# Side work placed by DMA time as well, weights and values loaded through GpSimd's queue, values' high parts made on GpSimd

## The chip, the cores and the metric

The kernel runs on one core of a Trainium2 chip. The metric is device time in microseconds of one execution; smaller is better. The kernel before took 2106.71 us (median of 3 runs, 2103.33 to 2109.67).

In the profile, PE is TensorE (matmuls), PEld its weight loads, DVE is VectorE, ACT is ScalarE, POOL is GpSimd and SP is SyncE, which issues nearly all DMAs here; SPq stands for its queue.

## The reference

A squared-ReLU attention without softmax, a product with `u`, and a gated feed-forward layer with RMS norm, all in f32:

```python
scores = (1.0 / S) * np.matmul(z, z.transpose(0, 2, 1))   # z: 4 x 3008 x 64
attn = np.maximum(scores, 0.0) ** 2
out = np.matmul(attn, v)                                  # v: 4 x 3008 x 256
x = (u * out).reshape(B * S, D)                           # 12032 x 256
rms = np.sqrt(np.mean(x * x, axis=-1, keepdims=True) + 1e-06)
xn = x / rms * rms_g
g = xn @ w_gate                                           # 256 x 1536
silu = g * (1.0 / (1.0 + np.exp(-g)))
val = xn @ w_val
return (silu * val) @ w_out                               # 1536 x 256
```

## The kernel before

**Precision.** f32 products are made of reduced-precision (fp32r) matmuls: each operand is split into a high part (a cast) and a low part (the difference), and a product takes three matmuls: high times high, low times high, high times low. So every tile that PE reads has a "cast" and a "subtract" on some engine ahead of it: `vh` and `vl` are the two parts of the values v, `zst` holds both parts of z, `H` and `L` those of the attention weights.

**Attention.** Each of the 4 batches has 3008 columns of queries, taken as three pairs of 512-column blocks; that makes 12 pairs, numbered p = 0 to 11 (batch p // 3). "Second pairs" are p = 1, 4, 7, 10 and "third pairs" p = 2, 5, 8, 11. A pair walks over the 24 key tiles of its batch, one a step (`phase_a`). A step makes, for both blocks, the scores of the step after next (`emit_s`), the high and low parts of the next one (`emit_l`, lines 502 to 558), and the product of the present weights with v (`emit_av`, 12 matmuls for both blocks). z times z transposed is symmetric, so a pair stores weights that a later pair of the batch needs transposed (`kept`, `diag`: `keep_tile` and `keep_half`), and the later pair fetches them by a transposing DMA into one of 6 buffers `T` (`load_turned`, line 440, `load_half`, line 450). The later the pair, the more it fetches and the fewer score matmuls it has: a third pair fetches most of its weights.

**Feed-forward.** 12 blocks of 1024 tokens, 12 units each (`Unit`), each a seven-product scheme of combined gate and value weights (`wcomb`, `wu` when loaded) with combinations of x, then the product with w_out (`woh`, `wol`). While a block runs, the next block's norm and splits (`norm_jobs`, `split_jobs`) are put into its slots by `Beside.put`; a block has 36 slots.

**Side work.** While the attention runs, the next batch's z and v are loaded and split (`prep_stat`, `prep_v`), the weights are decoded from 64-bit floats (`decode`: a load, then an ACT `magnitude`, DVE bit operations, a POOL sum or split), the gate and value weights are combined (`prep_proj`: POOL `combine`s, ACT casts and POOL subtracts of the `put`s, and the stores to `wcomb`), and w_out is split (`prep_wout`).

**What sets the order.** Everything is recorded in program order; each engine works its instructions off in that order and waits at the first one that isn't ready. Where a piece of side work stands is chosen beforehand: `plan_loads` adds up, per step, the cost of the main work on DVE (`d`), ACT (`a`) and POOL (`g`); `put` (lines 1056 to 1071) takes for each piece the first step at which its engine has room; `plan_batch` (lines 1097 to 1119) does it for a batch's z and v, with the step by which each is needed. DMA time has no account of its own, and every load and store of this side work is an issue of SP, among the transposing loads.

Of the kernel before, what the change touches and what calls it, by code (L numbers as in the profile page):

```python
# [19 lines left out]
P = 128  # L20
# [10 lines left out]
def kernel(  # L31
# [120 lines left out]
    def decode(src, a, square, into):  # L152
# [48 lines left out]
    def prep_wout(f):  # L201
# [7 lines left out]
        tiles, load, ops = decode(rows, 2, square, lambda: "woh2" if f in (0, 4) else "x6")  # L209
# [17 lines left out]
    def prep_proj(j, pool, tags):  # L227
# [16 lines left out]
        def put(o, value):  # L244
            def both():
# [121 lines left out]
    def prep_v(b, g, place="start"):  # L367
        k0 = 2 * g
        r0 = b * S + k0 * P
        tiles = {}  # L370

        def load():
            view = tiles["raw"] = new_raw(place).rearrange("p (a d) -> p a d", a=2)
            if k0 + 2 < NK:
                nc.sync.dma_start(out=view, in_=v[r0:r0 + 2 * P, :].rearrange("(a p) d -> p a d", p=P))
            else:
                nc.sync.dma_start(out=view[:, 0, :], in_=v[r0:r0 + P, :])
                for h in range(2):
                    nc.sync.dma_start(out=view[h * TAIL:(h + 1) * TAIL, 1, :], in_=v[r0 + P:r0 + P + TAIL, :])
# [628 lines left out]
    load_of = {e: [0.0] * STEPS for e in "dag"}  # L1008
    span_of = [0.0] * STEPS

    def plan_loads():
# [5 lines left out]
        for p in range(NPAIR):  # L1017
            b, c0 = where(p)[:2]
            d = a = 0.0
            for i in range(NK):  # L1020
                kt, g = order(p)[i], p * NK + i
                for k in range(2):
# [20 lines left out]
                    if kc > c and keeps(b, c, kc):  # L1043
                        add("d", g - 1, 0.69)
                        d += 0.69
                    if kc == c and c and p > 0 and kt % 4 < 2:
                        add("d", g, 0.4)
                        d += 0.4
                d, a = d + SIDE[p > 0][0], a + SIDE[p > 0][1]
            add("d", (p + 1) * NK - 1 if p < NPAIR - 1 else STEPS - 1, 2.8)  # L1050

    SIDE = (0.55, 0.45), (0.55, 0.1)
    FILL = 0.9
    plan_loads()

    def put(seq, start, last=None):

        g = start
        for e, cost, gap, fn in seq:
# [3 lines left out]
            near = lambda k: range(max(k - 1, 0), min(k + 2, STEPS))  # L1063
            room = lambda k: sum(FILL * span_of[x] - load_of[e][x] for x in near(k))
            fits = (k for k in range(g, end + 1) if (load_of[e][k] == 0 if e == "g" else room(k) >= cost))
            g = next(fits, None) if last is None else next(fits, max(range(g, end + 1), key=room))
            load_of[e][g] += cost
            if e == "g" and cost > 3:
# [28 lines left out]
    def plan_batch(b, places):  # L1097
# [3 lines left out]
        for c in range(NC):  # L1101
            used = [i - LA for i in range(NK) if order(prev)[i] // 4 == c and not all(is_turned(prev, i, k) for k in range(2))]
            free = (prev * NK + max(used) + 1) if used else prev * NK + 1
            need = min(i - LA for i in range(NK) if order(here)[i] // 4 == c) + here * NK - 1
            todo.append((min(need, here * NK + NK - 1), free, "d", prep_stat, c))
# [4 lines left out]
        todo.sort(key=lambda t: t[:2])  # L1110
# [21 lines left out]
    def plan_part(part, g, last=None):  # L1132
        load, ops = part
        at_step(g, load)
# [4 lines left out]
    for j in range(NF // 4):  # L1139
# [4 lines left out]
        g = put(ends, max(g, ended[-1])) + 1  # L1144
# [3 lines left out]
    places.update({f: ((batch - 1) * NP - 1) * NK + 1 for f in (4, 5)})  # L1148
    plan_batch(batch - 1, places)
    for f in range(0, NF, 2):  # L1150
        ended.append(plan_part(prep_wout(f), max(g, ended[-2 if f < 8 else -1] + 1, ended[-1] if f == 8 else 0)))
        g += 4
# [10 lines left out]

    for p in range(1, NM):
        m = Beside(p - 1)
# [95 lines left out]
```

## Time and profile before

| | us |
|---|---|
| median of 3 runs | 2106.71 |
| the profiled execution's own time | 2107.22 |
| span of its trace, first to last instruction | 2105.4 |
| attention, up to the last gate of pair 11 | 1039.2 |

The profile's page gives busy time by engine and 40 slices of the span. Stretches by pair are cut at the first product of a pair's result with `u` (line 631, DVE), so pair 2 is 176.3 to 265.3 us, pair 5 is 437.3 to 528.8, pair 8 is 698.2 to 790.4; pairs 3, 4 and 7 are 265.3 to 350.9, 350.9 to 437.3 and 613.8 to 698.2. What follows 1039.2 us is the feed-forward layer. An idle time of PE after which a matmul waits for ACT has to be followed to what ACT itself waited for, and that to the queue on which the late transfer stood.

### The profile page before, as it was taken

Reading aid. Unit: us, or ns where it says so; the run is one execution under the profiler, and the core shown is the slowest. Engines: PE = TensorE matmul, PEld = TensorE weight load, DVE = VectorE, ACT = ScalarE, POOL = GpSimd, SP = SyncE. Lnnn points to the kernel's source line nnn. Section 1 sums busy time; section 2 is a strip of 40 time slices with the busy share of each in tenths; the row PEclk is TensorE's granted clock in tenths of the full one; section 3 lists DMA queues with packets and bytes.
Section 4 is the critical chain, followed back from the end, with each engine's and each line's share of the span. In section 5 each row is a group of like instructions: output and inputs, shape, how many; then the busy total and the mean of one; then the engine's idle time right before and its main releaser. Section 6 shows DMA issues by size and latency. Waiting matters only on the chain.

```text
span 2105.4 us, 27047 instructions
## 1 busy us (share of the span) xinstructions
PE 2026.7 (96%) x8912; PEld 1673.2 (79%) x8912; DVE 1605.4 (76%) x2644; ACT 1370.5 (65%) x2588; POOL 253.8 (12%) x412
## 2 busy tenths in 40 slices
PE   9999799987999789998999999999999999999999
PEld 7888688776877668877888888888888888888889
DVE  7888578665787568876788878788787888878776
ACT  7776487644876548765567666676666667666665
POOL 1202621046103361111000000000000000000000
PEclk9999999998999899999999999999999999999999
DMA  2476857899568974597634344443434434344443
GB/s 77 134 194 148 208 178 204 208 209 233 179 174 202 245 192 163 171 215 180 191 131 163 123 163 148 136 163 123 159 126 160 161 124 161 123 160 143 137 154 121
DMA packets 391982, 346.47 MB, mean 165 GB/s; under 512 B 254944, under 2 KB 303968, under 8 KB 391840
## 3 DMA queue, kind: packets, MB, share of 16 engines
q1 hardware_dynamic: 391840, 344.73, 55.8%
q8 instruction: 70, 1.15, 0.2%
q14 instruction: 72, 0.59, 0.1%
HBM read 190.78 MB, written 94.77 MB: 136 GB/s over the span
## 4 chain that ended last, share of the span: by engine, by line
PE 49%; ACT 1%; DVE 1%; DMA 1%; issue 0%; ACTq 0%; SPq 0%; DVEq 0%
PE ps L808 10%; PE ps L809 10%; PE ps L810 10%; PE py L836 6%; PE py L840 6%; PE py L837 6%; ACT s L815 1%; PE po L595 0%; PE po L596 0%; PE po L600 0%; ACT hH L820 0%; DVE xl L774 0%; DVE s L905 0%; DVE x L774 0%; DMA wu<-wc 0%; ACT s L899 0%
## 5 line engine op out<-in xcount | busy, mean ns | idle before, releaser
L595 PE MATMUL po<-H,vh 128*128 128x512 f32 (+1 forms) x1152 | 461.4, 401 | 64.4 <-ACT H L514 42.0
L596 PE MATMUL po<-H,vl 128*128 128x512 f32 (+1 forms) x1152 | 454.7, 395 | 0.0
L815 ACT COPY s<-ps 128x512 f32<-128x512 f32 (+1 forms) x432 | 249.7, 578 | 194.6 <-PE ps L810 194.6
L600 PE MATMUL po<-L,vh 128*128 128x512 f32 (+1 forms) x1104 | 345.1, 394 | 4.5 <-DVE L L525 4.4
L595 PEld LDWEIGHTS po<-H,vh 128*128 128x128 f32 x1152 | 223.1, 194 | 124.9 <-ACT H L514 48.7
L525 DVE TENSOR_TENSOR L<-r,H 128x512 fp32r<-128x512 f32 (+1 forms) x302 | 202.7, 699 | 132.2 <-ACT r L519 111.6
L820 ACT CAST hH<-s 128x512 fp32r<-128x512 f32 (+1 forms) x288 | 176.7, 614 | 176.5 <-DVE s L905 174.8
L825 DVE TENSOR_TENSOR hL<-s,hH 128x512 fp32r<-128x512 f32 (+1 forms) x288 | 196.3, 682 | 121.2 <-ACT hH L820 109.2
L487 ACT ACTIVATE r<-ps 128x512 f32<-128x512 f32 x322 | 178.2, 594 | 164.9 <-PE ps L476 148.4
L596 PEld LDWEIGHTS po<-H,vl 128*128 128x128 f32 x1152 | 223.0, 194 | 41.0
L600 PEld LDWEIGHTS po<-L,vh 128*128 128x128 f32 x1104 | 210.4, 192 | 51.0 <-DVE L L525 11.1
L525 DVE TENSOR_TENSOR L<-T,H 128x512 fp32r<-128x512 f32 (+1 forms) x250 | 185.6, 777 | 55.8 <-ACT H L514 54.2
L836 PE MATMUL py<-hH,woh 128*128 128x512 f32 (+1 forms) x576 | 221.7, 385 | 0.3 <-ACT hH L820 0.3
L837 PE MATMUL py<-hH,wol 128*128 128x512 f32 (+1 forms) x576 | 221.6, 385 | 0.0
L808 PE MATMUL ps<-x,wu 128*128 128x512 f32 x504 | 197.4, 392 | 0.9 <-DMA wu<-wc 0.6
L809 PE MATMUL ps<-x,wu 128*128 128x512 f32 x504 | 196.3, 390 | 0.7 <-DMA wu<-wc 0.7
L810 PE MATMUL ps<-x,wu 128*128 128x512 f32 x504 | 196.3, 389 | 0.0
L808 PE MATMUL ps<-xh,wu 128*128 128x512 f32 (+1 forms) x504 | 192.8, 383 | 0.4
L810 PE MATMUL ps<-xl,wu 128*128 128x512 f32 (+1 forms) x504 | 191.6, 380 | 0.0
L809 PE MATMUL ps<-xh,wu 128*128 128x512 f32 (+1 forms) x504 | 191.6, 380 | 0.0
L840 PE MATMUL py<-hL,woh 128*128 128x512 f32 (+1 forms) x576 | 174.8, 385 | 0.0
L514 ACT CAST H<-T 128x512 fp32r<-128x512 f32 (+1 forms) x254 | 143.1, 600 | 26.8 <-PE po L596 21.1
(99 smaller groups left out, 3454.7 us busy)
## 6 DMA issues: line engine op xcount, KB each, us to landing
wu<-wc SPq DMA_DIRECT2D x288, 448.0 KB, 3.9
kept<-halves SPq DMA_DIRECT2D x197, 256.0 KB, 2.1
raw<-in_v SPq DMA_DIRECT2D x44, 256.0 KB, 4.0
ux<-xg SPq DMA_DIRECT2D x22, 512.0 KB, 5.4
out_T<-y SPq DMA_DIRECT2D x44, 256.0 KB, 2.2
raw<-in_zT SPq DMA_DIRECT2D x38, 256.0 KB, 3.6
ux<-in_uT SPq DMA_DIRECT2D x38, 256.0 KB, 3.4
xg<-ux SPq DMA_DIRECT2D x22, 256.0 KB, 2.1
```

What stands on the lines that cost most here:

```text
L525: nc.vector.tensor_tensor(lo[:, :n], a[:, :n], f32(hi[:, :n]), op=ALU.subtract)
L595: nc.tensor.matmul(po[d][:, :n], wh[:, j, ds], hi[:, :n], start=(i == 0), stop=False)
L596: nc.tensor.matmul(po[d][:, :n], wl[:, j, ds], hi[:, :n], start=False, stop=(ends and lo is None))
L600: nc.tensor.matmul(po[d][:, :n], wh[:, j, ds], lo[:, :n], start=False, stop=ends)
L808: nc.tensor.matmul(ps[:, :n], wh[:, o, :], xh[:, :n], start=start, stop=False, skip_group_check=True)
L809: nc.tensor.matmul(ps[:, :n], wl[:, o, :], xh[:, :n], start=False, stop=False, skip_group_check=True)
L810: nc.tensor.matmul(ps[:, :n], wh[:, o, :], xl[:, :n], start=False, stop=stop, skip_group_check=True)
L815: nc.scalar.copy(s, ps[:, :self.n])
L825: nc.vector.tensor_tensor(lo[:, :self.n], s, f32(self.h[h][0][:, :self.n]), op=ALU.subtract)
L836: nc.tensor.matmul(acc[h, d][:, :n], woh[f // 4][:, f % 4, ds], hi[:, :n], start=(f == 0), stop=False)
L837: nc.tensor.matmul(acc[h, d][:, :n], wol[f // 2][:, f % 2, ds], hi[:, :n], start=False, stop=False)
L840: nc.tensor.matmul(acc[h, d][:, :n], woh[f // 4][:, f % 4, ds], lo[:, :n], start=False, stop=(f == NF - 1))
```

## The change

Five things:

1. **Queues.** The weights' loads and the stores to `wcomb` are issued by GpSimd instead of SP, and so are v's loads from the second batch on.
2. **v's high part.** From the second batch on, `vh` is cast by GpSimd in four pieces of 128 columns instead of by ACT in one instruction.
3. **The planner** keeps a fourth account, `q`, for DMA time (the transposing loads, the stores of `kept` and `diag`, the loads of u and z), and a load or a weight's store looks for a step with room in it; the room that an engine may be filled to is set for each account.
4. **Places.** A batch's raw buffers may be used from the middle of the second pair on (before: from the start of the third), and the first two z blocks of batches 2 and 3 are made in the second pair. The last batch's v moves largely from pair 8 to pair 9.
5. **w_out.** Rows 8 to 11 of w_out's 12 (two decodes of six) move into the first block of the feed-forward layer, into `T` buffers.

```diff
@@ decode
-            raw = (keep if tag[0] == "w" else moving).tile([P, a, b, 2], U32, tag=tag, name="wraw")
-            nc.sync.dma_start(out=raw.rearrange("p a b c -> p a (b c)"), in_=src.bitcast(U32))
+            pool = work if tag == "T" else moving if tag[0] == "x" else keep
+            raw = pool.tile([P, a, b, 2], U32, tag=tag, name="wraw", bufs=6 if tag == "T" else 1)
+            nc.gpsimd.dma_start(out=raw.rearrange("p a b c -> p a (b c)"), in_=src.bitcast(U32))
@@ prep_proj, store
-                        nc.sync.dma_start(
+                        nc.gpsimd.dma_start(
@@ prep_v
+        queue = nc.gpsimd if b else nc.sync
...
-                nc.sync.dma_start(out=view, in_=v[r0:r0 + 2 * P, :].rearrange("(a p) d -> p a d", p=P))
+                queue.dma_start(out=view, in_=v[r0:r0 + 2 * P, :].rearrange("(a p) d -> p a d", p=P))
...
-            nc.scalar.copy(hi, tiles["raw"])
+            if b == 0:
+                nc.scalar.copy(hi, tiles["raw"])
+                return
+            for a in range(2):
+                for k in range(0, D, PIECE):
+                    nc.gpsimd.tensor_copy(hi[:, a, k:k + PIECE], tiles["raw"][:, a, k:k + PIECE])
@@ plan_loads
+                    if i % 2 == 0 and is_turned(p, i, k):
+                        add("q", g - 7, 2.2)
...
-    FILL = 0.9
+    FILL = dict(d=0.93, a=0.93, q=1.05, g=1.0)
@@ plan_batch
+            if c < 2 and b > 1:
+                free -= NK
...
+            s = put([("q", 0.8, 0, None)], s, max(need - 6, s))
             load, one, two = prep(b, n, place=place)
             at_step(s, load)
...
-            h = put([("a", 0.6, 0, one), (e, 0.7 if e == "d" else 2.4, 1, two)], max(s + 2, free), last)
+            if e == "d":
+                h = put([("a", 0.6, 0, one), ("d", 0.7, 1, two)], max(s + 2, free), last)
+            else:
+                h = put([("g", 2.4, 0, one), ("g", 2.4, 0, two)], max(s + 2, free), last)
...
-        plan_batch(b, {f: (b * NP - 1) * NK + 1 for f in range(NF // 2)})
+        plan_batch(b, {f: (b * NP - 2) * NK + 6 for f in range(NF // 2)})
@@ the first block of the feed-forward layer
+    beside = [Beside(p) for p in range(NM - 1)]
+    for f, h in zip(range(8, NF, 2), (5, 15)):
+        load, ops = prep_wout(f)
+        at(("M", 0), h, load)
+        for k, (e, cost, _, fn) in zip((3, 4, 5, 6, 7, 8), ops):
+            at(("M", 0), h + k, fn)
+            beside[0].room[e, h + k] = beside[0].room.get((e, h + k), 0.0) - cost
```

Three places show what this makes of the order. First ACT in pair 5; L383 is the cast of v's high part, L514 (L521 in the change, as lines have shifted) the cast of attention weights `H` from a fetched tile, L250 (L251) that of a combined weight, L359 that of z. Before:

```order
L514 CAST H<-T 128x448
L383 CAST vh_4973<-raw 128x512
L359 CAST zst_4975<-raw 128x512
L359 CAST zst_4977<-raw 128x512
L514 CAST H<-T 128x512
L514 CAST H<-T 128x448
L250 CAST wohi<-w_4215 128x512
```

In the change, about the same place:

```order
L251 CAST wohi<-ws 128x512
L521 CAST H<-T 128x512
L521 CAST H<-T 128x448
L521 CAST H<-T 128x512
L521 CAST H<-T 128x448
L521 CAST H<-T 128x512
L521 CAST H<-T 128x448
L494 ACTIVATE T<-ps 128x256
```

The casts of v are gone from ACT; two of z's have moved ahead.

Second POOL at the end of the gate and value weights (the third group of them, j = 2): `ws<-` and `w<-` of L144 are combinations, `wolo` the low parts, `wc` the stores. Before, in pairs 7 and 8:

```order
L144 TENSOR_TENSOR w_6312<-w_6312,w_6350 128x128 x4
L144 TENSOR_TENSOR wolo<-w_6310,wohi 128x128 x4
L144 TENSOR_TENSOR w_5303<-w_6312,w_5303 128x128 x4
L144 TENSOR_TENSOR wolo<-w_6312,wohi 128x128 x4
L144 TENSOR_TENSOR wolo<-w_5303,wohi 128x128 x4
L144 TENSOR_TENSOR ws<-w_6310,w_5303 128x128 x4
```

In the change, all in the second half of pair 8 (L390 is now the cast of v's high part, L401 its low part, L377 v's load):

```order
L144 TENSOR_TENSOR w_7210<-w_7210,w_7353 128x128 x4
L377 DMA raw<-in_v 128x2x256
L144 TENSOR_TENSOR wolo<-w_7085,wohi 128x128 x4
L390 CAST vh_7798<-raw 128x128 x4
L256 DMA wc_80<-wohi 128x4x128
L256 DMA wc_80<-wolo 128x4x128
L144 TENSOR_TENSOR w_7056<-w_7210,w_7056 128x128 x4
L144 TENSOR_TENSOR wolo<-w_7210,wohi 128x128 x4
L401 TENSOR_TENSOR vl_7864<-raw,vh_7798 128x128 x4
L256 DMA wc_80<-wohi 128x4x128
L256 DMA wc_80<-wolo 128x4x128
```

Between two combinations there now stand a load, a cast, a low part and the stores, all in one queue.

Third ACT at the end of the feed-forward layer's first block, where the next block's x is cast (L769, in the change L776; L820 and L827 cast `hH`, L815 and L822 copy scores). Before, in three places, the last of which reads:

```order
L815 COPY s<-ps 128x512
L899 ACTIVATE s<-s 128x512
L769 CAST xh<-ux_10571 128x512
L769 CAST xh<-xc 128x512
L820 CAST hH<-s 128x512
```

In the change, in one:

```order
L906 ACTIVATE s<-s 128x512
L776 CAST xh<-ux_10638 128x512
L776 CAST xh<-ux_10640 128x512
L776 CAST xh<-xc 128x512 x2
L776 CAST xh<-ux_10638 128x512
L776 CAST xh<-xc 128x512
L776 CAST xh<-ux_10640 128x512
L827 CAST hH<-s 128x512
```

All seven casts of the next block (and on DVE their seven subtracts) have come to stand in the block's last slot, ahead of the cast for the last unit's product.

## Rows read from the trace of the kernel before

**Rows 1.** The page: PE's busy time, its granted clock and DMA by slice.

```profile
PE 2026.7 (96%) x8912; PEld 1673.2 (79%) x8912; DVE 1605.4 (76%) x2644; ACT 1370.5 (65%) x2588; POOL 253.8 (12%) x412
...
PEclk9999999998999899999999999999999999999999
DMA  2476857899568974597634344443434434344443
```

**Rows 2.** Windows: pairs 2, 3, 4, 5, 7, 8, feed-forward (columns: PE, PEld, DVE, ACT, POOL).

```profile
176.30:265.30 89.00, 76.51 (x329) 63.75 (x328) 56.62 (x85) 50.13 (x99) 44.55 (x72) 0.94 0.79 194
265.30:350.90 85.60, 85.06 (x376) 69.81 (x375) 68.38 (x109) 67.33 (x128) 15.61 (x25) 1.00 0.57 179
350.90:437.30 86.40, 80.91 (x342) 64.91 (x341) 62.17 (x107) 52.92 (x102) 5.82 (x12) 0.96 0.85 206
437.30:528.80 91.50, 73.70 (x309) 60.11 (x308) 57.78 (x83) 46.89 (x91) 59.89 (x92) 0.91 0.91 226
...
613.80:698.20 84.40, 79.84 (x342) 64.64 (x341) 61.95 (x100) 52.70 (x102) 24.46 (x40) 0.96 0.78 197
698.20:790.40 92.20, 75.31 (x310) 59.98 (x309) 58.49 (x88) 47.06 (x92) 44.06 (x72) 0.93 0.89 219
...
1039.20:2105.40 1066.20, 1061.65 (x4768) 886.48 (x4767) 845.13 (x1431) 693.05 (x1293) 0.00 (x0) 1.00 0.42 145
```

**Rows 3.** Timeline of PE in pair 5 (start, length, idle time before and releaser).

```profile
479.26 0.80 PE L595 MATMUL po<-H,vh 128*128 128x512 f32 x1 [7.67 <-ACT H L514]
```

**Rows 4.** Timeline of ACT just before.

```profile
477.03 0.62 ACT L383 CAST vh<-raw 128x512 fp32r<-128x512 f32 x1 [10.39 <-DMA raw<-in_v]
```

**Rows 5.** Timeline of SP's queue just before.

```profile
468.15 5.05 SPq L440 DMA_TRANSPOSE T<-kept  x2
473.25 0.57 SPq L375 DMA_DIRECT2D raw<-in_v  x1
```

**Rows 6.** Waits of ACT over the whole span (total, times, longest).

```profile
ACT vh L383 <- DMA raw<-in_v: 71.6, 18, 10.4
...
ACT T L487 <- DMA T<-diag: 40.0, 8, 8.1
...
ACT w L168 <- DMA wraw<-in_w_val: 6.0, 1, 6.0
```

**Rows 7.** Waits of PE in pair 8.

```profile
PE po L595 <- ACT H L514: 6.5, 6, 2.1
PE po L595 <- ACT H L512: 5.4, 2, 4.9
PE po L595 <- DVE H L529: 2.7, 1, 2.7
```

**Rows 8.** Timeline of ACT in pair 7.

```profile
677.61 0.62 ACT L250 CAST wohi<-ws 128x512 fp32r<-128x512 f32 x1 [4.19 <-POOL ws L144]
```

**Rows 9.** Groups by line: POOL's side work, and the feed-forward splits (busy, mean ns).

```profile
L394 POOL TENSOR_TENSOR vl<-raw,vh 128x128 fp32r<-128x128 f32 x180 | 109.9, 641 | 242.6 <-ACT vh L383 119.7 <-PE po L600 59.4 <-DMA kept<-halves 31.9
...
L144 POOL TENSOR_TENSOR wolo<-w,wohi 128x128 fp32r<-128x128 f32 x60 | 38.6, 673 | 72.2 <-ACT wohi L250 72.2
...
L144 POOL TENSOR_TENSOR ws<-w,w 128x128 f32<-128x128 f32 x24 | 16.8, 728 | 0.0
...
L774 DVE TENSOR_TENSOR xl<-ux,xh 128x512 fp32r<-128x512 f32 (+1 forms) x24 | 15.9, 664 | 2.0 <-ACT xh L769 2.0
...
L221 POOL TENSOR_TENSOR wol<-wraw 128x128 fp32r<-128x128 f32 x24 | 13.7, 569 | 1.9
```

**Rows 10.** Groups of DVE by form, 575 to 615 us (no POOL at work).

```profile
L525 DVE TENSOR_TENSOR L<-T,H 128x512 fp32r<-128x512 f32 x4 | 2.7, 684 | 0.0
```

**Rows 11.** The same, 500 to 525 us, with POOL at work.

```profile
L525 DVE TENSOR_TENSOR L<-T,H 128x512 fp32r<-128x512 f32 x6 | 5.2, 868 | 0.1
```

**Rows 12.** DMA issues over the span (KB each, median us from issue to landing).

```profile
raw<-in_v SPq DMA_DIRECT2D x44, 256.0 KB, 4.0
...
wc<-wohi SPq DMA_DIRECT2D x21, 256.0 KB, 3.4
```

More of the change, by code (lines that the diff above doesn't have):

```diff
@@ L207, in square @@
             return woh[f // 4][:, f % 4:f % 4 + 2, :]
-        tiles, load, ops = decode(rows, 2, square, lambda: "woh2" if f in (0, 4) else "x6")
+        tiles, load, ops = decode(rows, 2, square, lambda: "woh2" if f in (0, 4) else "x6" if f < 8 else "T")
         def high():
@@ L1007 @@
     STEPS = NPAIR * NK
-    load_of = {e: [0.0] * STEPS for e in "dag"}
+    load_of = {e: [0.0] * STEPS for e in "dagq"}
     span_of = [0.0] * STEPS
@@ L1044, in plan_loads @@
                         add("d", g - 1, 0.69)
+                        add("q", g, 0.8)
                         d += 0.69
@@ L1047, in plan_loads @@
                         add("d", g, 0.4)
+                        add("q", g, 0.5)
                         d += 0.4
+                    if i % 2 == 0 and is_turned(p, i, k):
+                        add("q", g - 7, 2.2)
+                    elif i % 2 == 0 and is_half(p, i, k):
+                        add("q", g - 4, 1.5)
                 d, a = d + SIDE[p > 0][0], a + SIDE[p > 0][1]
             add("d", (p + 1) * NK - 1 if p < NPAIR - 1 else STEPS - 1, 2.8)
+            for n in range(4):
+                add("q", p * NK + 8 + 2 * n, 0.9)
+                add("q", min(p * NK + NK + n % 2, STEPS - 1), 0.9)
+            for n in range(2):
+                add("q", p * NK + 8 + 2 * n, 0.9)
     SIDE = (0.55, 0.45), (0.55, 0.1)
-    FILL = 0.9
+    FILL = dict(d=0.93, a=0.93, q=1.05, g=1.0)
     plan_loads()
@@ L1062, in put @@
             g = min(g, end)
-            near = lambda k: range(max(k - 1, 0), min(k + 2, STEPS))
-            room = lambda k: sum(FILL * span_of[x] - load_of[e][x] for x in near(k))
+            wide = 3 if e == "q" else 1
+            near = lambda k: range(max(k - wide, 0), min(k + wide + 1, STEPS))
+            room = lambda k: sum(FILL[e] * span_of[x] - load_of[e][x] for x in near(k))
             fits = (k for k in range(g, end + 1) if (load_of[e][k] == 0 if e == "g" else room(k) >= cost))
@@ L1067, in put @@
             load_of[e][g] += cost
+            if fn is None:
+                continue
             if e == "g" and cost > 3:
@@ L1103, in plan_batch @@
             free = (prev * NK + max(used) + 1) if used else prev * NK + 1
+            if c < 2 and b > 1:
+                free -= NK
             need = min(i - LA for i in range(NK) if order(here)[i] // 4 == c) + here * NK - 1
-            todo.append((min(need, here * NK + NK - 1), free, "d", prep_stat, c))
+            todo.append((need if free >= prev * NK else prev * NK + 1, free, "d", prep_stat, c))
         for g in range(NK // 2):
@@ L1109, in plan_batch @@
             todo.append((need, free, "g", prep_v, g))
-        todo.sort(key=lambda t: t[:2])
+        todo.sort(key=lambda t: (t[0] - 12, t[1]))
         for need, free, e, prep, n in todo:
@@ L1133, in plan_part @@
         load, ops = part
+        g = put([("q", 1.5, 0, None)], g)
         at_step(g, load)
@@ L1143 @@
             g += 4
-        g = put(ends, max(g, ended[-1])) + 1
+        g = max(g, ended[-1])
+        for end in ends:
+            if end[0] == "a":
+                g = put([("q", 1.6, 0, None)], g)
+            g = put([end], g)
+        g += 1
     assert g < STEPS - 2 * NK, g
@@ L1147 @@
     places = {f"x{h}{k}": here for k in range(4) for h in "hl"}
-    places.update({f: ((batch - 1) * NP - 1) * NK + 1 for f in (4, 5)})
+    places.update({f: ((batch - 1) * NP - 2) * NK + 6 for f in (4, 5)})
     plan_batch(batch - 1, places)
-    for f in range(0, NF, 2):
-        ended.append(plan_part(prep_wout(f), max(g, ended[-2 if f < 8 else -1] + 1, ended[-1] if f == 8 else 0)))
+    for f in range(0, 8, 2):
+        ended.append(plan_part(prep_wout(f), max(g, ended[-2] + 1)))
         g += 4
@@ L1162 @@
         put([("a", 0.6, 0, one), ("d", 0.7, 0, two)], last + 17, STEPS - 1)
+    beside = [Beside(p) for p in range(NM - 1)]
[5 more added lines that the diff above has]
+            beside[0].room[e, h + k] = beside[0].room.get((e, h + k), 0.0) - cost
     for p in range(1, NM):
-        m = Beside(p - 1)
+        m = beside[p - 1]
         at(("M", p - 1), 0, lambda p=p: load_x(p))
```

4 lines of the change are left out of this document (2 added, 2 removed).

## The prediction

> **What bounds the kernel now.** I read the page first, then windows by pair, then the timeline around PE's longest idle times, then the waits. PE is busy for 96% of the span, so the kernel is bound by PE, and what can be won is PE's idle time and the time in which its clock is low [rows 1]. The slices place both: the granted clock, a mean of its two levels of 1.2 and 2.4 GHz, dips in the 10th and 14th slice, where the DMA row stands at 9. The windows give this by pair [rows 2]. Pair 3 has 376 matmuls in 85.6 us at full clock, 0.2277 us each, with PE idle for half a microsecond; I take that as an undisturbed pair's rate. At it, the matmuls of pair 2 (329) would take 74.9 us, of pair 4 (342) 77.9, of pair 5 (309) 70.4, of pair 7 (342) 77.9, of pair 8 (310) 70.6. They take 89.0, 86.4, 91.5, 84.4 and 92.2: losses of 14.1, 8.5, 21.1, 6.5 and 21.6 us, 72 together. The feed-forward layer has 1061.65 us of PE in 1066.2 and gives nothing back.
>
> What lies behind a loss is seen in pair 5. PE stands for 7.67 us [rows 3]; ACT, which makes its `H`, had stood for 10.39 us on the cast of a v block for the next batch, which nobody needed yet [rows 4]; and this block's load had been issued only 3.8 us before it, behind two transposing loads that held SP's queue for 5.05 us [rows 5]. So a piece of side work that isn't urgent blocks ACT in its order, and the block comes from the place of its load in SP's queue. Over the span ACT loses 71.6 us in 18 such waits, 40.0 in 8 waits for the diagonal tile and 6.0 in one for `w_val` [rows 6]. PE feels such a wait less some 3 us: 10.39 became 7.67 [rows 3, 4]. The loss is then larger than PE's idle time, since the clock comes back late: in pair 8, 21.6 us of loss against 14.6 us of waits, a factor of 1.5 [rows 2, 7].
>
> **The change part by part.** *v's casts leave ACT, v's loads leave SP.* In pairs 2, 5 and 8 ACT no longer meets a load of v at all. What is late next there is the diagonal tile, which still comes by SP: 40.0 us in 8, 5.0 each, less 3, times 1.5, is 3 us in each of the three pairs. Pair 8 also loses the wait behind a w_out load (inside the 5.4 us) and that on z (2.7) [rows 7], as both move to other pairs. So 11 of 14.1, 18 of 21.1 and 18.6 of 21.6: 48 us. If the planner's spreading leaves one wait of 10 us standing, (10 - 3) x 1.5 = 10 come off.
>
> *The weights' loads.* Pair 4's wait on `w_val`, 6.0 us, is half of its loss: 4 us back. In pair 7 the `wcomb` stores no longer stand in SP's queue ahead of the diagonal load; of 6.5 us I take 3 (0 to 6.5). The new order puts a load behind a POOL sum of some 2.5 us (4 x 641 ns [rows 9]); ACT waits of up to 4 us are covered by what PE has in hand, as one of 4.19 us behind POOL in pair 7 shows: that pair's only long PE idle is elsewhere [rows 8]. So nothing; with the cover gone, three loads at (6 - 3) x 1.5 = 4.5 each, 13 us.
>
> That is 55 us. Now what the change adds.
>
> *POOL's queue in pair 8* is the largest item. From S3's low part to the combination S4, on which ACT's last weight cast waits, POOL has three more low parts (4 in all, 4 x 673 ns = 2.7 us each), three combinations (4 x 728 ns = 2.9), one low part of v (2.6) and two casts of v. Such a cast isn't in the trace: it reads one operand of 128 x 128 where the nearest rows read two, at 569 to 641 ns a piece [rows 9]; below I can't exclude anything down to nothing, and take 2.1 us for four. Sum 26 us. Nine DMA issues stand between them. What one holds POOL for isn't in the trace either: SP holds 0.57 us for a plain load [rows 5]; the far end is that POOL stands until the transfer lands, 3.4 to 4.0 us [rows 12]. I take 0.7, near SP's. The plan gives 8 steps of 12 matmuls, 8 x 2.73 = 21.9 us. So ACT waits 26 + 9 x 0.7 - 21.9 = 10.4 us in pair 8; less 3, times 1.5: 11 us. At 0 an issue with free casts it is nothing, at 3.4 it is 48. Behind ACT's cast stand all the casts of `H`, so PE feels it.
>
> *v in pair 9.* The plan now makes these blocks exactly two steps ahead of use. At the start POOL has 8 loads in a row, then a cast and a low part, 8 x 0.7 + 4.7 = 10.3 us, behind pair 8's last low part and its two stores (2.7 + 2 x 0.7 = 4.1 us), and PE needs the block after 4 steps of 16 matmuls, 14.6 us. It just fits; I put 2 us there (0 to 27 at 3.4 us an issue).
>
> *DVE beside POOL.* The same subtract takes 684 ns without POOL and 868 with it [rows 10, 11]. Pairs 3, 6 and 9 now have POOL at work for half their length, where DVE is busy 68.4 of 85.6 us [rows 2]. Half of 109 instructions at 0.18 us more is 10 us of DVE; 17 us of its idle time take it, but not evenly. I take 1 us a pair, 3 in all (0 to 9). The Trainium skill (SBUF — State Buffer, section "SBUF: two separate sides") says that GpSimd and a VectorE instruction with two SBUF inputs lock each other out for a whole instruction; the longer subtract agrees in kind, though its 184 ns are less than a whole POOL piece of 641, so the sum stays with the rows.
>
> *Feed-forward, first block.* Two w_out decodes add 10 DVE and 4 ACT instructions, which push the next block's seven subtracts into the last slot. There, five more than before, 5 x 0.66 = 3.3 us [rows 9], stand ahead of what the last unit's product needs. PE has no other work then: 4 us (0 to 9).
>
> *DMA.* Transposing loads stay in the third pairs and PE will use them faster; with v's loads spread and the last group's stores now in pair 8 I put 4 us (0 to 20, the second rival).
>
> Sum: 11 + 2 + 3 + 4 + 4 = 24 us against 55, so 31 us fewer. The profiled execution took 2107.22 us, 0.5 above the median; 2107.2 - 31 = 2076, and I say 2075.
>
> **The rivals.** *GpSimd's queue becomes the bound* (slower). Its mechanism is the one of pair 8: with d us an issue, pair 8 costs 1.5 x (1 + 9d), pair 9 max(0, 10d + 7.4 - 14.6) by the sums above, and 11 us are fixed. At d = 2.1 this eats the 55; at d = 2.5 it is 35 + 18 + 11 = 64, 2116 us; at 3.4 it is 85, 2137. Against it: SP's 0.57 us; for it: nothing bounds a GpSimd issue from above but the landing. The Trainium skill (the same page and section) warns that a DMA issued from GpSimd waits while VectorE copies in its faster modes, as GpSimd writes the descriptors; no run here shows a GpSimd issue, and by that rule d would be longer than SP's.
>
> *The transfers themselves are the bound.* DMA is busy 79 to 91% of the third pairs [rows 2], so a load issued earlier may only make another one late. In pair 8 the busy time is 0.89 x 92.2 = 82 us, in pair 5 83, in pair 2 70. If these pairs shrink only as transfers leave them (by the order some 11, 15 and 9 us' worth), 35 come back instead of 48, and the costs of 24 and the gains of 7 beside them leave 18: 2089 us. For it: slices at 9. Against it: ACT's waits name v's loads, and none names the transposing ones [rows 6]. The Trainium skill (DMA: Bandwidth & Descriptors, section "Issuing engines are not separate DMA queues") says that issuing from more engines saves only the sequencer's issue time; here that time is 5.05 us for two loads ahead of one that ACT waits for [rows 5], so even by that rule the wait goes.
>
> *The costs don't come.* POOL's lag stays under ACT's cover, and the full 55 and pair 7's rest come back: 2047 us.
>
> *The waits only change place.* ACT meets z and weights instead of v, and the planner's rooms don't hold at run time: 2100 to 2112, no change.
>
> **How the numbers follow.** The forecast has 0.56 (2058 to 2085 by its own terms), the transfers 0.16, no costs 0.10, changed place 0.08, GpSimd as the bound 0.10. A measurement tells 0.3%, 6.3 us, from no change. Faster: 0.56 + 0.16 + 0.10 less a little of the second for terms at their far ends, 0.81; same 0.08; slower 0.11. The range reaches from under the case without costs to the far side of changed places: 2040 to 2108.
>
> **What would show it.** Right: no wait of ACT for v after the first batch; pairs 2 and 5 near 75 us with the granted clock at 0.97 or more; waits of ACT for POOL's `ws` or `w` of about 10 us in pair 8; issues that hold POOL under 1 us; a PE gap of a few microseconds near the end of the first feed-forward block. Wrong: waits for T from `kept` where v's were (the transfers), or POOL idle on its own issues while PE waits for `vh` or `vl` in pair 9 (GpSimd's queue). If pairs 2 and 5 keep over 10 us of their losses, the account of rows 3 to 5 fails.

## The result and the profile after

The changed kernel takes 2116.86 us (median of 6 runs, 2108.57 to 2119.69) against 2104.92 for the kernel before (median of 6): a ratio of 1.0051, with a 95% interval of [1.0035, 1.0067]. It is slower by half a per cent, where 2075 had been forecast, and lies outside the range of 2040 to 2108. The page of its profiled execution (span 2115.0 us; the columns as in [rows 1]):

```profile
PE 2030.0 (96%) x8912; PEld 1675.3 (79%) x8912; DVE 1640.5 (78%) x2644; ACT 1354.9 (64%) x2552; POOL 361.8 (17%) x658
...
PEclk9999999999899999999999999999999999999999
DMA  2466856997369985588644344443434434344443
```

One dip of the clock is left of two, in the 11th slice, which is pair 6. DVE is busy 35 us longer than in [rows 1], with the same 2644 instructions. The windows by pair show what that costs. After, pairs 4 to 9 and the feed-forward layer (length; PE, PEld, DVE, ACT, POOL, each busy time with its instructions; then the granted clock, DMA share, GB/s):

```profile
348.10:439.80 91.70, 79.95 (x341) 64.00 (x341) 64.13 (x101) 55.36 (x105) 21.56 (x35) 0.94 0.88 215
439.80:516.50 76.70, 70.41 (x309) 59.11 (x308) 52.49 (x84) 38.05 (x74) 44.18 (x83) 0.96 0.86 205
516.50:616.20 99.70, 87.98 (x374) 71.17 (x374) 82.50 (x109) 66.50 (x127) 29.33 (x72) 0.93 0.51 160
616.20:702.20 86.00, 80.81 (x342) 65.13 (x341) 64.81 (x100) 55.33 (x106) 21.97 (x34) 0.96 0.85 229
702.20:779.30 77.10, 70.25 (x309) 59.45 (x308) 54.40 (x81) 40.33 (x78) 47.27 (x80) 0.96 0.86 195
779.30:875.70 96.40, 90.06 (x374) 69.40 (x373) 85.43 (x113) 67.62 (x129) 55.07 (x99) 0.98 0.64 201
...
1043.70:2115.00 1071.30, 1063.41 (x4768) 887.38 (x4766) 851.49 (x1441) 695.80 (x1297) 9.64 (x18) 1.00 0.42 145
```

Pairs 6 and 9 of before, which [rows 2] leave out:

```profile
528.80:613.80 85.00, 84.47 (x373) 69.30 (x373) 68.64 (x113) 67.98 (x129) 5.20 (x8) 1.00 0.59 182
790.40:875.40 85.00, 84.48 (x374) 69.33 (x373) 70.04 (x112) 67.50 (x129) 11.72 (x16) 1.00 0.55 170
```

The third pairs 5 and 8 gave back 14.8 and 15.1 us (91.5 and 92.2 in [rows 2]). The pairs behind them took as much: pair 6 is 14.7 us longer and pair 9 11.4, with as many instructions on DVE, give or take four, but 13.9 and 15.4 us more of its busy time. Pair 4 is 5.3 us longer instead of 4 shorter, and the feed-forward layer 5.1 longer. The cuts of [rows 2] don't all lie at the same point: 265.3 us is the start of pair 2's first product with `u`, most others are its end, some 0.6 us later, and 176.3 lies 0.9 us ahead of pair 1's. Cut at the start of the first product in both kernels, pair 2 goes from 88.1 to 83.0 us and pair 3 from 84.9 to 87.0; the other differences stay.

What happened in pair 6 stands in four engines' timelines (start, length, engine; idle time before and releaser in brackets):

```profile
538.07 1.29 DVE L532 TENSOR_TENSOR L<-r,H 128x512 fp32r<-128x512 f32 x2
539.28 13.31 DVE L581 COPY halves<-r 128x1024 uint16<-128x1024 uint16 x2
552.51 0.68 DVE L501 TENSOR_TENSOR r<-ps,r 128x512 f32<-128x512 f32 x1
...
538.60 0.73 POOL L377 DMA_DIRECT2D raw<-in_v  x1 [14.60 <-ACT r L526]
539.33 0.99 POOL L390 CAST vh<-raw 128x128 fp32r<-128x128 f32 x4
540.30 1.29 POOL L401 TENSOR_TENSOR vl<-raw,vh 128x128 fp32r<-128x128 f32 x3
...
552.08 0.60 ACT L494 ACTIVATE r<-ps 128x512 f32<-128x512 f32 x1 [10.18 <-DVE halves L581]
...
553.84 1.22 PE L607 MATMUL po<-L,vh 128*128 128x512 f32 x2 [10.35 <-DVE L L532]
```

One 16-bit copy of DVE, of 0.69 us elsewhere, took 12.7 us (13.31 with the next one). It began 0.05 us before the end of a DMA issue of POOL, and ended only when POOL's stretch of 36 further pieces without a pause was over (551.4). ACT waited for DVE, PE for both, and the granted clock of the pair is 0.93, where it was 1.00. In pair 9 the same comes in small, eight times, of 2.0 to 2.3 us each; once here:

```profile
816.12 0.68 DVE L532 TENSOR_TENSOR L<-r,H 128x512 fp32r<-128x512 f32 x1
816.72 2.04 DVE L532 TENSOR_TENSOR L<-T,H 128x512 fp32r<-128x512 f32 x1
...
814.50 2.44 POOL L390 CAST vh<-raw 128x128 fp32r<-128x128 f32 x4
816.92 2.15 POOL L401 TENSOR_TENSOR vl<-raw,vh 128x128 fp32r<-128x128 f32 x4
```

In the trace of before no DVE instruction takes over 1.2 us; after, 18 do, 54.6 us together. They are called long below. The one just shown ends at 818.76, ahead of GpSimd's last subtract (819.07): VectorE got its turn here without a pause of GpSimd, while in pair 6 it came only behind the pause.

Waits of ACT after, over the whole span (total, times, longest); of v's 71.6 us of [rows 6] only 2.6 are left, in the first batch, and the diagonal tile's have grown by 10:

```profile
ACT T L494 <- DMA T<-diag: 50.5, 7, 11.5
ACT H L521 <- PE po L603: 36.9, 51, 3.2
ACT r L494 <- DVE halves L581: 30.8, 14, 10.2
ACT H L521 <- DMA T<-kept: 17.2, 9, 3.6
```

### The profile page after: what moved, and what is told of

It is laid out like the page before. It is cut to its first block, busy times and chain, and to the rows that moved or that the text cites. A ratio compares the mean times of both kernels' runs of the same rounds, so it can differ in the third digit from the quotient of the medians.

```text
span 2115.0 us, 27190 instructions
## 1 busy us (share of the span) xinstructions
PE 2030.0 (96%) x8912; PEld 1675.3 (79%) x8912; DVE 1640.5 (78%) x2644; ACT 1354.9 (64%) x2552; POOL 361.8 (17%) x658
## 4 chain that ended last, share of the span: by engine, by line
PE 50%; ACT 1%; DVE 1%; DMA 0%; issue 0%; ACTq 0%; DVEq 0%
PE ps L815 10%; PE ps L816 10%; PE ps L817 10%; PE py L843 6%; PE py L844 6%; PE py L847 6%; PE po L607 1%; PE po L603 1%; ACT s L822 1%; PE po L602 1%; DVE xl L781 0%; DVE s L912 0%; ACT hH L827 0%; DMA wu<-wc 0%; DVE x L781 0%; ACT s L906 0%
## 5 line engine op out<-in xcount | busy, mean ns | idle before, releaser
L822 ACT COPY s<-ps 128x512 f32<-128x512 f32 (+1 forms) x432 | 249.8, 578 | 194.5 <-PE ps L817 194.4
L532 DVE TENSOR_TENSOR L<-r,H 128x512 fp32r<-128x512 f32 (+1 forms) x302 | 220.2, 757 | 92.9 <-ACT r L526 72.1
L827 ACT CAST hH<-s 128x512 fp32r<-128x512 f32 (+1 forms) x288 | 176.8, 614 | 179.4 <-DVE s L912 177.7
L815 PE MATMUL ps<-x,wu 128*128 128x512 f32 x504 | 197.5, 392 | 1.6 <-DMA wu<-wc 1.3
L815 PE MATMUL ps<-xh,wu 128*128 128x512 f32 (+1 forms) x504 | 193.2, 383 | 3.2 <-DVE s L912 2.9
L521 ACT CAST H<-T 128x512 fp32r<-128x512 f32 (+1 forms) x254 | 145.4, 601 | 62.2 <-PE po L603 36.9
```

The source lines that it names most:

```text
L532: nc.vector.tensor_tensor(lo[:, :n], a[:, :n], f32(hi[:, :n]), op=ALU.subtract)
L815: nc.tensor.matmul(ps[:, :n], wh[:, o, :], xh[:, :n], start=start, stop=False, skip_group_check=True)
L822: nc.scalar.copy(s, ps[:, :self.n])
```

## The experiments

Experiments 1, 11 and 12 are small kernels of their own; all others start from the changed kernel. GpSimd does two new things in it, issues and casts; the experiments take them apart. Ratios are to the kernel before, with 95% intervals.

**1. Two streams by themselves.** A kernel in which 30 subtracts on VectorE run beside different streams of GpSimd.

```python
def dve(n=30):
    for _ in range(n):
        nc.vector.tensor_tensor(lo, a, f32(h), op=ALU.subtract)          # 128x512
phase([]); phase([subs] * 8); phase([casts, subs] * 6); phase([twos, subs] * 5)
phase([issue, subs] * 6); phase([casts] * 12); phase([issue] + [subs] * 8); phase([casts] + [subs] * 8)
```

> Computes nothing of the reference: seven times, 30 subtracts of 128x512 back to back on VectorE (0.69 us each alone) stand beside a stream of GpSimd instructions of 128x128, with both engines meeting ahead of each. Theory A (VectorE is starved where GpSimd goes from a one-input cast or a DMA issue to a two-input subtract): beside 32 subtracts the two engines take turns, no VectorE instruction over 1.2 us; beside groups of 4 casts and 4 subtracts, and of a DMA issue and 4 subtracts, about one of 1.5 to 2.5 us in each of the 6 groups; beside 4 two-input copies (x - 0) and 4 subtracts, none; beside casts alone, none; behind one issue, or 4 casts, with 32 subtracts, one of up to 14 us. Rival B (any unbroken stretch of GpSimd work slows VectorE alike): the same mean in all stretches of two-input work, 0.9 to 1.1 us, and none over 1.5.

Measured: the windows of the first three and of the two with issues (DVE, ACT, POOL; the few extra instructions are the meetings):

```profile
1.30:25.80 24.50, 20.78 (x32) 1.93 (x3) 0.29 (x2) 1.00 0.06 21
25.80:53.10 27.30, 24.68 (x33) 0.00 (x0) 26.93 (x34) 1.00 0.00 0
53.10:83.20 30.10, 22.68 (x32) 0.00 (x0) 29.82 (x50) 1.00 0.00 0
...
113.50:142.80 29.30, 28.28 (x32) 0.00 (x0) 18.99 (x32) 1.00 0.18 54
...
169.20:204.00 34.80, 33.81 (x32) 0.00 (x0) 14.51 (x35) 1.00 0.03 8
```

Beside 32 subtracts the engines take turns: 0.83 us an instruction of DVE, 0.90 a piece of POOL. Behind one issue, POOL does the same 32 at 0.45 us each, and one DVE instruction takes 13.75 us. In the six groups with an issue three take 2.57, behind every second issue. Behind the others the engines take turns, though GpSimd made no pause; its four subtracts then take 3.05 us instead of 1.69:

```profile
114.28 0.85 POOL L67 DMA_DIRECT2D load<-in_v  x1
115.15 1.69 POOL L54 TENSOR_TENSOR vl<-raw,vh 128x128 fp32r<-128x128 f32 x4
116.79 0.72 POOL L67 DMA_DIRECT2D load<-in_v  x1
117.53 3.05 POOL L54 TENSOR_TENSOR vl<-raw,vh 128x128 fp32r<-128x128 f32 x4
```

The three long instructions began 0.08 to 0.09 us before the end of an issue, those that took turns 0.13 to 0.14 us after it. Casts made none: half of theory A falls here, and so does B.

**2. Two inputs instead of a cast** (index expressions shortened).

```diff
-                    nc.gpsimd.tensor_copy(hi[:, a, k:k + PIECE], tiles["raw"][:, a, k:k + PIECE])
+                    nc.gpsimd.tensor_tensor(hi[...], tiles["raw"][...], zeros.to_broadcast([P, PIECE]), op=ALU.subtract)
```

> The high part of v is made by GpSimd as raw - 0 (two inputs) instead of as a cast (one input), at the same places and from the same queue. Theory A (starvation where GpSimd goes from one input to two): the 8 long VectorE instructions of pair 9 that begin beside a cast (2.0 us each instead of 0.69) become turns of 0.95, 8 x 1.1 = 9 us off pair 9 (96.4 to about 88); that of 12.7 us in pair 6 begins beside a DMA issue and may stay; total about 2108 against 2116.9. Rival B (GpSimd's amount of work is what counts): a piece takes 0.45 instead of 0.28 us, so pairs 6 and 9 get longer by 0 to 3 us, 2117 to 2122. Rival C (v comes late by GpSimd's queue): no change, 2115 to 2119.

Measured: 2128.86 us, 1.0112 [1.0099, 1.0125]; 19 long instructions, 75.0 us. Theory A expected pair 9 to recover; it took 110.1 us, and this stood in it:

```profile
816.73 18.32 DVE L535 TENSOR_TENSOR L<-r,H 128x512 fp32r<-128x512 f32 x1
```

So the change from a cast to two inputs isn't the cause. The long copy of pair 6, over 36 pieces as before, takes 14.66 us instead of 12.71: longer pieces make a longer wait. The 18.32 us cover 46 pieces up to GpSimd's next pause, where with casts VectorE had come in after three.

**3. The cast by ACT again.**

```diff
-            if b == 0:
+            if True:
                 nc.scalar.copy(hi, tiles["raw"])
                 return
```

> The cast of v's high part goes back to ACT, at the places where GpSimd had it; loads stay on GpSimd's queue. Theory A: no change from one input to two is left except behind DMA issues, and each low part waits for ACT's cast, which breaks GpSimd's runs: pair 6 from 99.7 to about 87 and pair 9 from 96.4 to about 88, together 20 us, less up to 10 where ACT waits for v again in the third pairs: 2097 to 2107. Rival B: the work on GpSimd falls by the casts (about a third of v's), pairs 6 and 9 shorter by some 8 together: 2109. Rival C: the loads are as late as before, pairs 6 and 9 keep their length: 2115 or more.

Measured: 2092.09 us, 0.9934 [0.9913, 0.9956]: faster than before, and faster than any theory had it (A from 2097). Pairs 6 and 9:

```profile
515.50:601.00 85.50, 84.97 (x374) 69.39 (x373) 73.60 (x109) 69.44 (x133) 31.69 (x48) 1.00 0.59 187
764.80:852.70 87.90, 85.10 (x373) 69.18 (x373) 75.29 (x114) 72.50 (x139) 42.53 (x60) 1.00 0.71 223
```

Eight long instructions are left (30.1 us), all beside issues of weights' stores. Pair 8 stays at 75.7 us though ACT casts again: v's casts needn't have left ACT. C falls.

**4. v's loads by SP, the cast by GpSimd.**

```diff
-        queue = nc.gpsimd if b else nc.sync
+        queue = nc.sync
```

> v's loads go back to SP's queue, casts stay on GpSimd, places as in the change. Theory A: the 12.7 us in pair 6 (begins beside the issue of such a load) goes or falls to groups of 2 us, pair 9 keeps its 8 instructions of 2 us, as they begin beside casts: pair 6 about 88 to 92, pair 9 about 95, total 2105 to 2110, if SP's queue is not blocked by a load that waits for its buffer (14.6 us on GpSimd in pair 6; on SP that would hold up the transposing loads, and pairs 3 and 6 would get longer). Rival C: both pairs fall to about 87, total 2095. Rival B: both pairs stay, 2115.

Measured: 2111.06 us, 1.0027 [1.0015, 1.0039]; 22 long instructions (56.4 us); pair 6 at 92.9, pair 9 at 95.6, close to what A said. The weights are still issued by GpSimd, one of them 7.0 us before pair 9's first instruction of 2.0 us.

**5. The stores by SP**, cast by ACT: in the store of the combined weights `nc.gpsimd.dma_start` becomes `nc.sync.dma_start`.

> v's high part cast by ACT (as in the last-but-one experiment, 2092 us) and the stores of the combined weights issued by SP again; the loads of v and of the weights stay on GpSimd's queue. Theory A (a VectorE instruction that comes while GpSimd is in a DMA issue is passed over by all that GpSimd does next): all 8 VectorE instructions over 1.2 us begin beside such a store (30 us together), so none is left; PE feels only that of 6.2 us in pair 8 (4.2 us idle): total 2084 to 2090. Rival B (amount of work): no change in them, 2092. Rival D (SP's queue): 42 more issues of 0.6 us on SP stand ahead of the diagonal tile's load, pairs 4 and 7 get longer by 2 to 4 us each: 2094 to 2100.

Measured: 2090.85 us, 0.9935 [0.9914, 0.9956]. The eight long instructions are gone, three others (9.4 us) stand behind v's issues. The time is the same as in 3, so what the eight cost can't be told in it.

**6. The weights' loads by SP too**: the same edit in `decode`.

> As the one before, and the weights' loads are issued by SP too; only v's loads stay on GpSimd's queue. In pair 4 the wait for the diagonal tile is 12.7 us with the cast on ACT (7.3 before the change), behind transposing loads that held SP for 5.8 and 8.4 us beside a weight's load from GpSimd's queue. If a load from the other queue is what stretches them, pair 4 falls by 4 to 8 us: 2082 to 2088. If the place that the planner gives to the weights' loads does it (now 10 to 15 us nearer to the diagonal tile), pair 4 stays near 95 and the total at 2086 to 2094.

Measured: 2085.31 us, 0.9903 [0.9883, 0.9923]. Pair 4 falls from 98.6 us in the kernel of 5 to 87.3:

```profile
344.50:431.80 87.30, 80.01 (x342) 64.49 (x341) 61.55 (x100) 54.97 (x106) 17.47 (x24) 0.96 0.87 215
```

This is no chance of one profile: pair 4 takes 91.7 to 98.6 us in the six kernels whose weights' loads are on GpSimd's queue, 85.5 to 87.3 in the four where SP issues them. The longest that a transposing load of `kept` holds SP is 8.6 to 13.4 us in those six and 5.3 to 6.0 in those four. What the loads do there is seen in SP's queue. The last transposing load ahead of the diagonal tile's, after:

```profile
416.63 5.11 SPq L447 DMA_TRANSPOSE T<-kept  x1
```

And before:

```profile
415.45 2.76 SPq L440 DMA_TRANSPOSE T<-kept  x1
```

After, a weight's load had been issued by POOL 1.5 us earlier, at 415.1.

**7. The places alone**: cast by ACT, every issue by SP; only the planner, the places and w_out's move remain.

> Of the change only the planner, the places and w_out's move are left: v's high part is cast by ACT and every load and store is issued by SP. If the places alone bring the gain of the third pairs (36 us in pairs 2, 5 and 8), they stay at 75 to 80 us and the total is 2082 to 2095. If the queue brings it (v's loads behind transposing loads on SP), ACT waits for v in the third pairs again: 10 to 30 us are lost there, 2100 to 2115. Theory A: no VectorE instruction over 1.2 us either way, since GpSimd issues no DMA and casts nothing.

Measured: 2089.14 us, 0.9925 [0.9908, 0.9943], no long instruction. Pairs 4, 6 and 9:

```profile
347.10:432.80 85.70, 79.28 (x341) 63.96 (x340) 61.51 (x100) 55.08 (x105) 17.47 (x24) 0.96 0.86 221
514.00:599.30 85.30, 84.77 (x373) 69.22 (x372) 71.42 (x108) 69.22 (x132) 27.81 (x40) 1.00 0.59 187
761.30:849.10 87.80, 85.09 (x374) 69.17 (x374) 74.65 (x114) 72.49 (x139) 30.99 (x41) 1.00 0.70 215
```

Pairs 2, 5 and 8 take 83.9, 81.2 and 73.0 us, 33.7 less than before, against 35.0 less in the changed kernel. So the places bring nearly all of these pairs' gain, and neither the queue nor the cast is needed for it. ACT still waits for v, though less than the 71.6 us of before (total, times, longest):

```profile
ACT vh L386 <- DMA raw<-in_v: 30.9, 8, 7.5
```

**8. w_out back in the attention**, with the cast by ACT: `for f in range(0, NF, 2)` as before, nothing in the first feed-forward block.

> v's high part cast by ACT, and all six decodes of w_out made in the attention again (none in the first block of the feed-forward layer); queues as in the change. The feed-forward layer was 5 to 7 us longer with two of them, with a PE idle of 2.9 us at its first block's end; this goes: 2092 - 5 = 2087 if pairs 9 to 11 (88.0, 85.5 and 85.5 us with the cast on ACT) have room for them, and 2092 or more if they don't.

Measured: 2089.40 us, 0.9926 [0.9902, 0.9949], not to be told from 3; five long instructions (16.1 us), all begun at the end of an issue. The feed-forward layer falls by 6.8 us (1072.0 to 1065.2), and pair 11 grows by 3.9 (83.5 to 87.4).

**9. The cast on GpSimd, with every issue by SP.**

> The places of the change with every load and store on SP, and v's high part cast by GpSimd: beside the run with the places alone (2089 us, no VectorE instruction over 1.2 us) only the engine of this cast differs. Theory A (the cast on GpSimd starves VectorE, whatever queue issues the loads): 10 to 15 VectorE instructions over 1.2 us, all beside a cast or the first pieces behind it, pairs 3, 6 and 9 longer by 5 to 10 us each (85.3, 85.3 and 87.8 with ACT): 2102 to 2115. Rival C (GpSimd's queue and its issues are what cost): as the places alone, 2085 to 2093.

Measured: 2093.31 us, 0.9933 [0.9919, 0.9946], no long instruction, though GpSimd has all of v's casts and subtracts. Pairs 6 and 9, with about as much POOL work as after:

```profile
514.50:600.10 85.60, 84.71 (x373) 69.22 (x372) 69.63 (x109) 66.37 (x126) 33.36 (x56) 1.00 0.60 185
764.70:851.20 86.50, 85.02 (x374) 69.17 (x374) 76.56 (x114) 67.60 (x129) 52.81 (x80) 1.00 0.71 217
```

Theory A, that the cast starves VectorE whatever queue issues, falls, and so does B, that the amount of GpSimd's work is what counts. With the changed kernel, 3 and 7 it makes a square: cast by ACT, issues by SP 0.9925; GpSimd's issues alone 0.9934; its cast alone 0.9933; both 1.0051. The cost lies in having both.

**10. The two best together**: 6, with w_out as in 8.

> Cast by ACT, weights' loads and stores by SP, v's loads by GpSimd's queue (2085 us), and w_out wholly in the attention (3 us in the run before, inside the uncertainty). Sum of the two: 2082, 2079 to 2088; if p9 to p11 have no room for w_out, 2085 or more. No VectorE instruction over 1.2 us but the two or three behind v's issues (9 us together).

Measured: 2086.71 us, 0.9910 [0.9894, 0.9926], two long instructions. The same as 6, which stays the lowest, though its interval overlaps those of 7 and 10.

**11. The streams beside a mixed VectorE**: the kernel of 1, with VectorE's products out of PSUM and 16-bit copies among the subtracts.

> Computes nothing of the reference: GpSimd's streams of 128x128 pieces (32 subtracts; 6 times 4 casts and 4 subtracts; 5 times 4 two-input copies and 4 subtracts; 3 times an issue and 4 subtracts) beside two mixes of VectorE: product out of PSUM and subtract in turn, then product, subtract, subtract of 448 columns and two 16-bit copies. With subtracts alone on VectorE only the issue starved it (2.57 us), the cast did not. Theory A2 (VectorE loses its turn behind any GpSimd instruction without two inputs, if it comes at the wrong moment, which needs its own instructions that don't share the port, as out of PSUM): subtracts or copies of 2.0 us beside casts in one mix or both, none over 1.2 beside 32 subtracts. Rival E (casts starve nothing, the 2.0 us in pair 9 have another cause): none over 1.2 us but behind the issues.

Measured: beside casts, copies and subtracts no instruction over 0.94 us; the only long one (2.08 us) stands behind an issue, one of six in this kernel. A2 falls, E holds here.

**12. What opens the state.** All 80 long instructions of the eight timed kernels in which GpSimd issues, counted from their traces, stand in a stretch of GpSimd work without a pause of 0.1 us and with an issue ahead in that stretch, up to 33 us back. The three kernels without such issues (before, 7, 9) have 37, 56 and 42 such stretches of over 2.5 us, and no long instruction. In the eight kernels 214 stretches of over 2.5 us have no issue and no long instruction either. But an issue alone doesn't make one: of the 167 stretches of that length with an issue, 49 hold a long instruction. And only 7 of the 80 lasted up to the pause; in the other 73 VectorE came in while GpSimd went on.

```python
phase("s", [issue] + [subs] * 8);               phase("s", [issue, landed] + [subs] * 8)
phase("s", [issue, subs, landed] + [subs] * 7); phase("s", [subs] * 2 + [issue] + [subs] * 6)
phase("s", [issue] + [casts, subs] * 5);        phase("ps", [issue] + [casts, subs] * 5)
phase("pstcc", [issue] + [casts, subs] * 5);    phase("s", [issue] + [twos, subs] * 4)
# landed: GpSimd reads what the issue loads; "ps", "pstcc": the mixes of 11
```

> Computes nothing of the reference. So far every VectorE instruction over 1.2 us (80 in eight kernels) stands in a stretch of GpSimd work without a pause that has a DMA issue ahead in it, and stretches without an issue have none. Theory A3: the issue opens this state, a pause ends it. So, beside 30 subtracts on VectorE: behind an issue with 32 subtracts one of about 13.8 us; with a wait for the transfer's landing between issue and subtracts none over 1.2 us; with 4 subtracts, then this wait, one of up to 2.6 us and none after it; with 8 subtracts ahead of the issue, turns before it and one of about 10 us behind it; behind an issue with groups of 4 casts and 4 subtracts, or 4 two-input copies and 4 subtracts, several of 1.5 to 14 us, while without an issue these groups had none. Rival F (only the instruction that comes during the issue itself is passed over; later casts don't matter): at most one long instruction in each stretch, and the wait for the landing makes no difference to a later one.

Measured, the windows in this order (DVE, ACT, POOL):

```profile
26.10:61.10 35.00, 34.01 (x33) 0.00 (x0) 14.65 (x35) 1.00 0.03 8
61.10:89.60 28.50, 24.24 (x33) 0.00 (x0) 25.88 (x36) 1.00 0.03 9
89.60:117.30 27.70, 25.92 (x31) 0.00 (x0) 26.84 (x36) 1.00 0.03 9
117.30:150.10 32.80, 31.79 (x31) 0.00 (x0) 17.62 (x35) 1.00 0.03 8
150.10:184.10 34.00, 33.01 (x32) 0.00 (x0) 15.89 (x43) 1.00 0.03 8
184.10:208.00 23.90, 23.90 (x33) 0.00 (x0) 18.37 (x43) 1.00 0.03 11
208.00:233.40 25.40, 24.98 (x33) 0.00 (x0) 22.78 (x43) 1.00 0.04 10
233.40:268.20 34.80, 33.81 (x33) 0.00 (x0) 14.47 (x35) 1.00 0.02 8
```

And the first long instruction in the timeline of DVE, and what stands at the same place where GpSimd paused for the landing:

```profile
27.68 13.84 DVE L58 TENSOR_TENSOR lo<-a,h 128x512 fp32r<-128x512 f32 x1
...
65.53 2.69 DVE L58 TENSOR_TENSOR lo<-a,h 128x512 fp32r<-128x512 f32 x3
```

Most points came as A3 had them. Behind the issue one instruction takes 13.84 us; after a pause none takes over 0.97. With four pieces ahead of the pause one takes 2.21, and turns follow. In mid-stretch there are turns of 0.82 to 0.97 before the issue, and one of 10.56 behind it. With casts in the stream two take 11.02 and 2.55, with two-input copies one takes 13.72. In both mixes each of the five groups of casts and subtracts behind an issue gives one of 1.83 us, where 11 had none without an issue. That is pair 9's pattern, and F falls.

A3 is too simple in one point: a pause ends the state, but it isn't the only thing that does. The 11.02 us ended in a cast, 3.5 us ahead of the pause, most of those of 1.83 in the next group's first cast, and in experiment 1 turns came back behind a second issue.

## Why the prediction was wrong, point by point

**The step that failed is "DVE beside POOL"**, put at 1 us a pair, 3 in all, with 9 as its far end. The three pairs (3, 6 and 9) got longer by 28 us: 2.1, 14.7 and 11.4. The step named the right engines and pairs, but took its price, 0.18 us an instruction, from rows in which POOL and DVE take turns [rows 10, 11]. In the kernel before they always do (no DVE instruction takes over 1.03 us), and POOL issues no DMA there. Behind an issue of its own GpSimd can fail to give the turn, and one instruction of VectorE then waits for a run of GpSimd's pieces, at worst for all of them up to the next pause. The added casts made these runs longer and free of pauses: with ACT's cast each low part waits for ACT, and the longest stretch of GpSimd falls from 46.9 to 23.4 us (experiment 3). So two edits, each of which costs nothing that can be told, cost 25 us together (1.0051 against 0.9933 and 0.9934, experiment 9's square). The prediction priced the edits one by one. Without this step the change would have come to 2089 to 2093 us (experiments 3, 7 and 9), inside the range and still 14 to 18 above the forecast.

The Trainium skill (SBUF — State Buffer, section "SBUF: two separate sides") has the port held for a whole instruction by whichever engine started first. The turns agree in kind only: 32 pieces beside 30 subtracts take 26.3 us, 0.82 a turn, less than 0.69 and 0.45 one after the other. The 12.7 us of 36 pieces do not agree; there the measurement decides.

**v's waits** (48 forecast). They went, but gave back 35 us: pairs 5 and 8 gained 14.8 and 15.1 us against 18 and 18.6, pair 2 5.1 against 11. Pair 2 keeps 8.1 us of its loss and pair 5 6.3, under the 10 that was to be the sign against this account, but the granted clock stayed at 0.94 and 0.96. Reading the waits from the place of a load in the queue [rows 4, 5] was right; but the new places bring the gain by themselves, not the queue or the cast (experiment 7). The diagonal tile was underrated as what is late next: 50.5 us of ACT's waits instead of 40.0 [rows 6].

**The weights' loads** (7 forecast, 4 in pair 4 and 3 in pair 7). Pair 4 lost 5.3 instead. The loads now lie nearer to the diagonal tile's, and from GpSimd's queue they run beside a transposing load, which held SP nearly twice as long; with SP as issuer the loss goes (experiments 5 and 6). Why pair 7 lost 1.6 is not settled: it is no shorter with SP as issuer (90.1 and 89.0 us in experiments 6 and 7).

**POOL's queue in pair 8** (11) cost nothing. ACT's wait for POOL's combinations there is 0.4 us. The issue was sized well (0.53 to 0.89 us, 0.7 taken); the four casts take 1.0 us where POOL is alone, not 2.1, and POOL's pieces 0.45 instead of 0.64 to 0.73 wherever DVE gives way. **v in pair 9** (2): PE waits nowhere for `vh` or `vl`, so POOL wasn't late. In the seven experiments without a long instruction in this pair it still takes 86.4 to 87.9 us against 85.0, so 1 to 3 us of its loss come with the work moved there, and the rest is DVE's.

**The feed-forward block** (4) is 5.1 us longer, with a wait of PE just where it was put:

```profile
1132.81 0.72 PE L815 MATMUL ps<-xh,wu 128*128 128x512 f32 x1 [2.89 <-DVE s L912]
```

**The rivals.** "GpSimd's queue becomes the bound" gave 2116 us at 2.5 us an issue. The time came out there, the mechanism didn't: an issue takes 0.53 to 0.89 us. A number was hit by chance. The Trainium skill (SBUF — State Buffer, section "SBUF: two separate sides") warns that a GpSimd issue waits while VectorE runs one of its faster copies. None of 102 issues held GpSimd over 0.89 us, and it was VectorE that waited; whether such a wait is part of the later landing (5.5 us against 4.0), no run here shows. "The costs don't come" adds up to 2049 by its own terms (2107.2 less 55 and 3.5), not 2047; nothing hangs on it.

**The sum.** 42 us were missed (2117 against 2075). 25 are the failed step's (28 instead of 3, with the 1 to 3 us of pair 9 in them). The rest nearly cancels: 13 less from v, 9 in pair 4, 5 in pair 7, 1 in the feed-forward layer and 4 in pairs 10 and 11, which no step had priced, against 17 forecast for POOL's queue, v in pair 9 and the DMA's share, of which the pairs show nothing beyond what is counted here. 2 are left over. With the cuts at one point the prediction's undisturbed pair 3 takes 84.9 us, not 85.6; that moves none of its losses by more than 0.7 us.

## What to carry to other kernels

Where GpSimd computes beside VectorE, look at the longest VectorE instructions, not at their mean, and at what GpSimd did last before them. Don't let GpSimd issue DMAs in a stretch in which it goes on computing: let SP issue them, as in the kernels of experiments 7 and 9, or let GpSimd wait for the landing behind each issue, which only the stream of experiment 12 shows. Price edits that meet on one resource together, since two that are free alone can cost 25 us as a pair.

## What the hardware showed that was not expected

- Behind a DMA issue by GpSimd, VectorE can lose its turns: 13.84 us instead of 0.69 behind one issue and 32 pieces, up to 18.32 in a kernel. Without an issue, or after a pause, the two take turns (0.83 and 0.90 us an instruction). It doesn't happen behind every issue (49 of 167 stretches), and VectorE often comes in again without a pause (73 of 80). Why the issue does that, and when it does not, no run here settles; in experiment 1 an instruction that began 0.08 us before the issue's end was passed over, one that began 0.13 us after it was not.
- It reaches far: an instruction of 2.04 us stood 33 us behind the last issue (experiment 4), in a stretch without a pause.
- GpSimd gains what VectorE loses: 32 subtracts in 13.2 us instead of 26.3.
- Beside a load from GpSimd's queue a transposing load held SP for 5.11 us instead of 2.76, and in the six kernels with such loads the longest held it for 8.6 to 13.4 us, against 5.3 to 6.0 in four without; an issue by GpSimd of 256 KB lands after 5.5 us (median of 33), by SP after 4.0 [rows 12].
